# Casting weights inside their transfers: the last input-weight slice and all output weights go to fp16 on the way in, issued by GpSimd

## The chip, the cores and the metric

The kernel runs on one core of one Trainium2 chip. A core has a matrix engine (TensorE, PE in the profile), a vector engine (VectorE, DVE), an activation engine (ScalarE, ACT), a general engine (GpSimd, POOL) and a queue engine (SyncE, SP) that only issues transfers. ACT and POOL can issue transfers too, each on a queue of its own; all queues are worked off by the same 16 DMA engines. The metric is the device time of one execution in microseconds, taken as the median of several runs. A profile is one such execution, recorded.

## What is computed

A linear-attention recurrence (retention) over four batches of 768 tokens with 8 heads of 64, then one feed-forward block on all 3072 tokens. Cut to what matters:

```python
gamma = 1.0 - 2.0 ** (-5.0 - np.arange(H))          # H = 8, D = 64, S = 768, B = 4
for t in range(S):
    state = gamma * state + einsum('bhd,bhe->bhde', k[:, :, t], v[:, :, t])
    y[:, :, t] = einsum('bhd,bhde->bhe', q[:, :, t], state) / sqrt(D)
x = y.transpose(0, 2, 1, 3).reshape(B * S, H * D)    # 3072 x 512
h = x @ w_in                                         # w_in 512 x 2048
g = h * tanh(softplus(h))                            # mish
out = g @ w_out                                      # w_out 2048 x 512
```

All inputs and the output are fp32 in DRAM; the matrix products are done on fp16 operands.

## The kernel before

The tokens are cut into 24 chunks of 128 (a batch has six). A chunk's recurrence is done as matrices: scores k·q under a mask of decays (`scores`, `mask`), the outer product that updates the state (`outer`, `state`), and the output as a part from the present chunk and a part from the state (`present`, `past`, together `y_two`). For that q and k must lie transposed. Chunks 4 and 5 are turned by PE (`turn`), later ones by a transposing transfer (`turn_by_dma`). The casts of q and v to fp16, with the decay factors, are GpSimd's (`cast_q`, `cast_v`), that of k is ScalarE's (`cast_k`).

The feed-forward works in blocks. Block 0 has four chunks (512 tokens) and is done by plain products; the later ones have two chunks each. In block 0 the first product goes in 16 steps (`g1`, u = 0 to 15, four matmuls each, the two first in halves by `first_g1`), each followed by the mish activation on ScalarE; the second product has 16 steps more (`g2_mm`, w = u - 16, four matmuls each). From block 1 on (first product) and block 2 on (second product) a scheme with seven half-size products in place of eight is used, which needs sums and differences of weights, built once: `win_sums` from input-weight slices 0 and 2, `weight_sums` from output-weight slices 0 and 2 (half 0) and 1 and 3 (half 1). These are VectorE's, put in a list called `late` and taken from it at given places by `some_late`.

The weights come in slices. `w_in` has four slices of 512 columns (slice s serves steps u = 4s to 4s + 3, each of its two halves two steps). `w_out` has four slices of 512 rows (slice s serves w = 4s to 4s + 3). Before, each slice of 1 MiB is brought as fp32 into a staging buffer by SP's queue (`load_w`, L145 to L158; the last output slice in two halves by `load_last_wout`, L160 to L163) and cast to a resident fp16 tile: the first half slice by GpSimd, the other input slices and output slices 0 to 2 by VectorE (`cast_win`, L165; `cast_wout`, L171), output slice 3 by ScalarE. The staging pool has four buffers, also used by the first q and later by the sums, so a transfer may wait until a buffer's last reader is done. Output slices 2 and 3 are staged in another pool.

The order of all work is written by hand: each engine executes its instructions in the order in which the program names them, and waits by semaphores for what they read. What sets the order around the change:

- SP's queue at the start (`first_block`, L804): first q, the k and v of chunks 0 to 3, then `load_weights` (L777): the input slices, output slices 0 to 2, then q and v of chunk 4.
- The dictionary `plan` (L885): work to be named after step u of block 0. `load_more` (L787, after u = 15) issues k of chunk 4 and q and v of chunk 5 on ScalarE's queue, where they stand behind the activation of step 15, and on SP's queue k of chunk 5, the last output slice and the loads of chunks 6 and 7.
- The last lines of the loop over u (L914 to L918): the buffers of the weight sums and the sums themselves.

`gate` (L346) is a one-column copy by GpSimd into a scratch tile; it makes what follows on that queue wait for the tile that it reads.

```python
16: [(cast_wout, 2), (load_more,), (casts, CPB)],
23: [(casts, CPB + 1), (cast_wout, 3, True)],
24: [(turn, CPB)],
25: [(scores_one, CPB)],
27: [(turn, CPB + 1)],
```

Here CPB is 4: chunk 4 is turned after step u = 23, chunk 5 after u = 26.

Of the kernel before, what the change touches and what calls it, by code (L numbers as in the profile page):

```python
# [9 lines left out]
FP16 = mybir.dt.float16  # L10
FP32 = mybir.dt.float32
# [5 lines left out]
def kernel(  # L17
# [9 lines left out]
    nc = tc.nc  # L27
    B, H, S, D = q.shape
    d_model, d_ff = moe_w_in.shape
    P = 128  # L30
# [4 lines left out]
    TB = 512  # L35
    CPB = TB // C
# [4 lines left out]
    NFB = d_ff // P  # L41
# [41 lines left out]
    gcm = cpool.tile([P, HP, P], FP32, name="gcm")  # L83
    warm = cpool.tile([P, 1], FP32, name="warm")
    gate_t = cpool.tile([P, 1], FP16, name="gate")
    nc.gpsimd.memset(ident, 0.0)
    nc.gpsimd.affine_select(
        out=ident, in_=ident, compare_op=ALU.not_equal, fill=1.0, base=0,
# [53 lines left out]
            load(nload[0])  # L142
            nload[0] += 1

    def load_w(which, s):  # L145
        if which == "in":
            t = wstage.tile([P, NBP, TB], FP32, name="wi", tag="wt", bufs=4)
            n = TB // 2 if s < 2 else TB
            for o in range(0, TB, n):
                nc.sync.dma_start(t[:, :, o:o + n], win_ap[:, :, s * TB + o:s * TB + o + n])  # L150
        else:
            if s < NSL // 2:
                t = wstage.tile([P, FPS, d_model], FP32, name="wt", tag="wt", bufs=4)
            else:
                t = gp.tile([P, FPS, d_model], FP32, name="wt", tag="g")
            if s < NSL - 1:
                nc.sync.dma_start(t, wout_ap[:, s * FPS:(s + 1) * FPS])
        wtmps[which, s] = t  # L158

    def load_last_wout(half):  # L160
        f = slice(half * (FPS // 2), (half + 1) * (FPS // 2))
        nc.sync.dma_start(
            wtmps["out", NSL - 1][:, f], wout_ap[:, NFB - FPS + f.start:NFB - FPS + f.stop])  # L163

    def cast_win(s, half, eng):  # L165
        src = wtmps["in", s]
        t = cpool.tile([P, NBP, TB // 2], FP16, name=f"win{s}_{half}")
        eng.tensor_copy(t, src[:, :, half * (TB // 2):(half + 1) * (TB // 2)])
        wins[s, half] = t

    def cast_wout(s, on_act=False):  # L171
        src = wtmps.pop(("out", s))
        t = cpool.tile([P, FPS, d_model], FP16, name=f"wout{s}")
        if on_act:
            for f in range(0, FPS, 2):
                nc.scalar.copy(t[:, f:f + 2], src[:, f:f + 2])
        else:
            nc.vector.tensor_copy(t, src)
        wouts[s] = t

    def store(n):
        for _ in range(n):
# [163 lines left out]
    def gate(x):  # L346
        nc.gpsimd.tensor_copy(gate_t, x)  # L347
# [6 lines left out]
    def at_tile():  # L354
        return atps.tile([P, 2, HP // 2, R, C], FP32, name="at", tag="at")
# [180 lines left out]
    def some_late(n):  # L536
        for _ in range(min(n, len(late))):
            late.pop(0)()
# [236 lines left out]


    def load_weights():  # L777
        for s in range(NSL):
            load_w("in", s)
        for s in range(NSL):  # L780
            load_w("out", s)
        room(CPB)
        room(CPB + 1)
        load_one(CPB, 0, nc.sync)
        load_one(CPB, 2, nc.sync)

    def load_more():  # L787
        load_one(CPB, 1, nc.scalar)
        load_one(CPB + 1, 0, nc.scalar)
        load_one(CPB + 1, 2, nc.scalar)  # L790
        load_one(CPB + 1, 1, nc.sync)
        load_last_wout(0)
        load_last_wout(1)
        nload[0] += 2
        load_to(CPB + 4)

# [7 lines left out]
    def first_block():  # L804
# [49 lines left out]
        for half in range(2):  # L854
            cast_two("v", 1, half)
        cast_win(0, 0, nc.gpsimd)
        at = at_tile()
        scores_half(1, 1, at)
        mask_half(1, 1, at)
# [16 lines left out]
        state_first(3)  # L876
        for s in range(1, NSL):
            for half in range(2):
                cast_win(s, half, nc.vector)
            if s == 2:  # L880
                late.extend(win_sums())
            if s >= 2:
                some_late(4)
        room_for_sums()
        plan = {  # L885
            9: [(cast_wout, 0)],
            12: [(cast_wout, 1)],
            16: [(cast_wout, 2), (load_more,), (casts, CPB)],
            23: [(casts, CPB + 1), (cast_wout, 3, True)],
            24: [(turn, CPB)],  # L890
            25: [(scores_one, CPB)],
            27: [(turn, CPB + 1)],
# [5 lines left out]
        for u in range(2, 2 * NFB):  # L898
            if u < NFB:
                g1(0, u)  # L900
            elif u < 2 * NFB - 2:
                w = u - NFB
                for t in range(CPB):
                    if w == 0:
                        o_tiles[t] = mmps.tile([P, d_model], FP32, name="o_ps", tag="mm")
                    g2_mm(o_tiles[t], 0, t, w)
            else:
                for t in range(CPB // 2) if u % 2 == 0 else range(CPB // 2, CPB):
                    for w in range(NFB - 2, NFB):
                        g2_mm(o_tiles[t], 0, t, w)  # L910
                    g2_out(o_tiles[t], 0, t, 1, on_act=t == CPB - 1)
            for fn, *args in plan.get(u + 1, ()):
                fn(*args)
            if u == NFB - 1:  # L914
                room_for_more()
                late.extend(weight_sums(0) + weight_sums(1))
            if NFB <= u < NFB + 5:
                some_late(1)  # L918
        hsnaps.append(gp.tile([P, 4, TB], FP32, name="hsnap", tag="g0"))

# [122 lines left out]
```

## Time and profile before

| what | value |
|---|---|
| median of three runs | 204.29 us (203.35 to 204.36) |
| the profiled execution | 203.41 us |
| its span, first to last instruction | 201.2 us |
| PE busy | 193.6 us, 96% |
| VectorE, ScalarE, GpSimd busy | 142.3, 111.2, 68.1 us |
| transfers | 38.65 MB, mean 192 GB/s |
| granted PE clock | 1.000 |

In the profile's lines a group reads: line, engine, operation, output <- inputs, shapes and count. In a timeline each line starts with the start and the duration in microseconds, and ends, in brackets, with the idle time of the engine just before and with what ended it. SPq and ACTq are issues of transfers; the transfer itself lands later. In the table by stretches a row has the stretch, then PE's busy time, its count of matmuls, the granted clock, the DMA engines' share and GB/s. In the chart of 40 slices a digit is the busy share of a slice of 5 us in tenths.

### The profile page before, as it was taken

What the parts mean: (1) busy time and instruction counts of PE and PEld (TensorE: products, weight loads), DVE (VectorE), ACT (ScalarE), POOL (GpSimd) and SP (SyncE); (2) the same over time, 40 slices, a digit from 0 to 9 for tenths busy, and PEclk for the clock granted to TensorE, in tenths of its full rate; (3) what the DMA queues carried; (4) which work ended last, traced back from release to release, by engine and by line L of the source; (5) the groups of instructions that cost most, each with busy time, mean ns of one, the idle gap of its engine ahead of it and who ended that gap; (6) DMA issues with size and microseconds to landing.
All of it is one profiled execution on the core that took longest, in us unless ns stands there. A gap on an engine that the chain in (4) does not pass through costs nothing.

```text
span 201.2 us, 5425 instructions
## 1 busy us (share of the span) xinstructions
PE 193.6 (96%) x2239; PEld 152.5 (76%) x2239; DVE 142.3 (71%) x271; ACT 111.2 (55%) x199; POOL 68.1 (34%) x83
## 2 busy tenths in 40 slices
PE   6897999999999999999999999999999999999993
PEld 2355544455965888988988988988988988988982
DVE  2787793958839696787696695787696695595552
ACT  2363665243970874674674674674664763753840
POOL 4072000529324417514407607603406616200000
PEclk9999999999999999999999999999999999999999
DMA  5999999999999999997992993999993923200202
GB/s 169 302 312 359 385 387 302 271 263 205 210 180 269 279 221 195 199 227 166 215 194 72 232 230 73 232 190 153 241 200 57 235 81 55 104 3 30 79 26 78
DMA packets 95896, 38.65 MB, mean 192 GB/s; under 512 B 82304, under 2 KB 89984, under 8 KB 95872
## 3 DMA queue, kind: packets, MB, share of 16 engines
q1 hardware_dynamic: 92608, 37.50, 84.3%
q10 hardware_dynamic: 3264, 0.82, 2.3%
q8 instruction: 17, 0.28, 0.6%
q14 instruction: 7, 0.06, 0.1%
HBM read 27.30 MB, written 6.29 MB: 167 GB/s over the span
## 4 chain that ended last, share of the span: by engine, by line
PE 91%; ACT 2%; DMA 2%; DVE 2%; issue 1%; DVEq 0%
PE o_ps L727 28%; PE h_ps L656 18%; PE h_ps L632 16%; PE o_ps L519 10%; PE h_ps L497 6%; PE y_ps L436 3%; PE at L386 3%; DMA qfirst<-in_q_dram 2%; PE y_ps L426 2%; PE u_ps L400 2%; ACT xt L482 1%; PE h_ps L800 1%; DVE qfirst L204 1%; DVE am L274 1%; ACT qk L235 1%
## 5 line engine op out<-in xcount | busy, mean ns | idle before, releaser
L656 PE MATMUL h_ps<-xt,win 128*128 128x256 f16 x320 | 41.2, 273 | 0.0
L329 POOL TENSOR_TENSOR qk<-qf,qvs 128x512 f16<-128x512 f32 x20 | 24.1, 1207 | 25.3 <-DMA qf<-in_q_dram 23.4
L656 PEld LDWEIGHTS <-win 128*128 128x128 f16 x320 | 29.3, 98 | 3.7
L727 PEld LDWEIGHTS <-gsum 128*128 128x128 f16 x288 | 27.5, 98 | 4.0
L649 DVE TENSOR_TENSOR hsum<-h_ps,hsnap 128x512 f32<-128x512 f32 x30 | 19.8, 688 | 13.7 <-PE h_ps L632 11.5
L392 DVE TENSOR_TENSOR am<-at,tri 128x1024 f16<-128x1024 f32 x20 | 24.2, 1217 | 3.9 <-PE at L386 3.9
L660 ACT ACTIVATE g<-h_ps 128x512 f16<-128x512 f32 x40 | 23.7, 593 | 5.6 <-PE h_ps L656 5.5
L727 PE MATMUL o_ps<-tmat,gsum 128*128 128x256 f16 x216 | 25.1, 273 | 0.0
L639 ACT COPY hsnap<-h_ps 128x512 f32<-128x512 f32 x30 | 16.6, 588 | 13.9 <-PE h_ps L632 13.9
L338 POOL TENSOR_TENSOR v<-vf,qvs 128x512 f16<-128x512 f32 x20 | 21.3, 1064 | 5.3 <-PE u_ps L400 3.9
L727 PEld LDWEIGHTS <-g 128*128 128x128 f16 x216 | 21.1, 98 | 2.5
L741 DVE TENSOR_TENSOR osb<-o_ps,snap 128x256 f32<-128x256 f32 x27 | 11.4, 424 | 16.1 <-PE o_ps L727 11.3
L519 PE MATMUL o_ps<-wout,g 128*128 128x512 f16 x96 | 22.7, 380 | 0.0
L643 ACT ACTIVATE g<-hsum 128x512 f16<-128x512 f32 x30 | 18.7, 634 | 4.0 <-DVE hsum L649 4.0
L482 ACT CAST xt<-y_ps 128x1024 f16<-128x1024 f32 x10 | 10.1, 1012 | 19.1 <-PE y_ps L436 19.1
L632 PEld LDWEIGHTS <-wsum 128*128 128x128 f16 x320 | 19.1, 98 | 0.5
L733 ACT COPY snap<-o_ps 128x256 f32<-128x256 f32 x27 | 10.0, 372 | 15.7 <-PE o_ps L727 15.7
L334 ACT ACTIVATE qk<-kf 128x512 f16<-128x512 f32 x20 | 12.7, 633 | 8.4 <-DMA kf<-in_k_dram 8.4
L727 PE MATMUL o_ps<-wout,g 128*128 128x256 f16 x144 | 17.2, 273 | 0.0
L632 PE MATMUL h_ps<-xsum,wsum 128*128 128x128 f16 x240 | 16.7, 219 | 0.0
L347 POOL COPY gate<-gsum 128x1 f16<-128x1 f16 x8 | 1.5, 186 | 44.2 <-DVE gsum L701 44.2
L632 PEld LDWEIGHTS <-win 128*128 128x128 f16 x240 | 15.1, 98 | 1.5 <-issue 0.8
(96 smaller groups left out, 288.3 us busy)
## 6 DMA issues: line engine op xcount, KB each, us to landing
kf<-in_k_dram SPq DMA_DIRECT2D x23, 256.0 KB, 4.4
vf<-in_v_dram SPq DMA_DIRECT2D x23, 256.0 KB, 5.5
out_dram<-osb SPq DMA_DIRECT2D x22, 256.0 KB, 4.3
qf<-in_q_dram SPq DMA_DIRECT2D x19, 256.0 KB, 4.5
wt<-in_moe_w_out_dram SPq DMA_DIRECT2D x3, 1024.0 KB, 8.7
wi<-in_moe_w_in_dram SPq DMA_DIRECT2D x4, 512.0 KB, 7.2
wi<-in_moe_w_in_dram SPq DMA_DIRECT2D x2, 1024.0 KB, 11.1
qfirst<-in_q_dram SPq DMA_DIRECT2D x2, 512.0 KB, 5.2
```

The source lines that it names most:

```text
L329: nc.gpsimd.tensor_tensor(room16(g)[0], loaded[g][0], qs.unsqueeze(2).broadcast_to((P, H, D)), op=ALU.mult)
L334: nc.scalar.mul(room16(g)[1], loaded[g][1], BOOST)
L338: nc.gpsimd.tensor_tensor(room16(g)[2], loaded[g][2], vs.unsqueeze(2).broadcast_to((P, H, D)), op=ALU.mult)
L392: nc.vector.tensor_tensor(am, ats.pop(g), tri.unsqueeze(1).unsqueeze(1).broadcast_to((P, 2, HP, C)), op=ALU.mult)
L519: nc.tensor.matmul(o_ps, gts[blk, fb][:, t * P:(t + 1) * P], wouts[s][:, f, cols], start=(fb == 0), stop=(fb == NFB - 1))
L632: nc.tensor.matmul(h_ps[:, f], w(f, d), x(d), start=first and f == 0 and d == 0, stop=d == n - 1, skip_group_check=True)
L639: nc.scalar.copy(x, h_ps)
L643: nc.scalar.activation(gt[:, 2 * i * FPS:(2 * i + 1) * FPS, j * P:(j + 1) * P], h, AF.Mish, scale=inv_boost3)
L649: nc.vector.tensor_tensor(h, h_ps, x, op=ALU.add)
L656: nc.tensor.matmul(h_ps[:, j], win(s, 2 * half + j, bp), xt(blk, bp), start=bp == 0, stop=bp == NBP - 1)
L660: nc.scalar.activation(gt[:, fb:fb + 2], h_ps, AF.Mish, scale=inv_boost3)
L727: nc.tensor.matmul(o_ps, x(f), w(f), start=first and f == 0, stop=f == n - 1, skip_group_check=True)
```

## The change

A transfer that GpSimd issues may change the type of what it moves. The change uses this for the last input slice (two transfers, one per half) and for all four output slices: the fp16 tiles are written by the transfers directly, with no staging buffer and no cast by an engine.

On GpSimd's queue, behind the cast of the first half slice, stands a gate on the second half of input slice 1; then the two halves of input slice 3 and output slices 0, 2 and 1, in this order. Output slice 3 is issued after step u = 15, between the cast of q and that of v of chunk 4. On SP's queue, behind input slice 2, stands a transfer of one element out of output slice 2's tile (`gate_d`), so that the loads of q and v of chunk 4, now named in `load_more`, and all behind them wait for that slice. The sums of output slices 0 and 2 are named after step u = 11 (four at once), those of slices 1 and 3 from step u = 24 on.

```diff
+    gate_d = cpool.tile([1, 1], FP16, name="gate_d")
...
-    def load_w(which, s):
...
-    def load_last_wout(half):
...
+    def load_win(s):
+        t = wstage.tile([P, NBP, TB], FP32, name="wi", tag="wt", bufs=4)
+        n = TB // 2 if s < 2 else TB
+        for o in range(0, TB, n):
+            nc.sync.dma_start(t[:, :, o:o + n], win_ap[:, :, s * TB + o:s * TB + o + n])
+        wtmps[s] = t
+
+    def bring_win(s, half):
+        t = wins[s, half] = cpool.tile([P, NBP, TB // 2], FP16, name=f"win{s}_{half}")
+        o = s * TB + half * (TB // 2)
+        nc.gpsimd.dma_start(t, win_ap[:, :, o:o + TB // 2])
+
+    def bring_wout(s):
+        t = wouts[s] = cpool.tile([P, FPS, d_model], FP16, name=f"wout{s}")
+        nc.gpsimd.dma_start(t, wout_ap[:, s * FPS:(s + 1) * FPS])
...
-    def cast_wout(s, on_act=False):
...
     def load_weights():
-        for s in range(NSL):
-            load_w("in", s)
-        for s in range(NSL):
-            load_w("out", s)
+        for s in range(NSL - 1):
+            load_win(s)
+
+    def bring_weights():
+        gate(wtmps[1][:, 0, TB // 2:TB // 2 + 1])
+        for half in range(2):
+            bring_win(NSL - 1, half)
+        for s in (0, 2, 1):
+            bring_wout(s)
+
+    def load_more():
+        nc.sync.dma_start(gate_d, wouts[2][:1, 0, :1])
         room(CPB)
         room(CPB + 1)
         load_one(CPB, 0, nc.sync)
         load_one(CPB, 2, nc.sync)
-
-    def load_more():
         load_one(CPB, 1, nc.scalar)
         load_one(CPB + 1, 0, nc.scalar)
         load_one(CPB + 1, 2, nc.scalar)
         load_one(CPB + 1, 1, nc.sync)
-        load_last_wout(0)
-        load_last_wout(1)
         nload[0] += 2
         load_to(CPB + 4)
...
         cast_win(0, 0, nc.gpsimd)
+        bring_weights()
...
         for s in range(1, NSL):
             for half in range(2):
-                cast_win(s, half, nc.vector)
+                if s < NSL - 1:
+                    cast_win(s, half, nc.vector)
...
         plan = {
-            9: [(cast_wout, 0)],
-            12: [(cast_wout, 1)],
-            16: [(cast_wout, 2), (load_more,), (casts, CPB)],
-            23: [(casts, CPB + 1), (cast_wout, 3, True)],
+            16: [(load_more,), (cast_q, CPB), (bring_wout, NSL - 1), (cast_k, CPB), (cast_v, CPB)],
+            23: [(casts, CPB + 1)],
...
-            if u == NFB - 1:
+            if u == NFB - 5:
                 room_for_more()
-                late.extend(weight_sums(0) + weight_sums(1))
-            if NFB <= u < NFB + 5:
+                late.extend(weight_sums(0))
+                some_late(4)
+            if u == NFB + 8:
+                late.extend(weight_sums(1))
                 some_late(1)
```

More of the change, by code (lines that the diff above doesn't have):

```diff
@@ L143, in load_to @@
             nload[0] += 1
-    def load_w(which, s):
[L146 to L158, printed above, removed]
-    def load_last_wout(half):
-        f = slice(half * (FPS // 2), (half + 1) * (FPS // 2))
-        nc.sync.dma_start(
-            wtmps["out", NSL - 1][:, f], wout_ap[:, NFB - FPS + f.start:NFB - FPS + f.stop])
+    def load_win(s):
[11 more added lines that the diff above has]
+        nc.gpsimd.dma_start(t, wout_ap[:, s * FPS:(s + 1) * FPS])
     def cast_win(s, half, eng):
-        src = wtmps["in", s]
+        src = wtmps[s]
         t = cpool.tile([P, NBP, TB // 2], FP16, name=f"win{s}_{half}")
@@ L169, in cast_win @@
         wins[s, half] = t
-    def cast_wout(s, on_act=False):
[L172 to L179, printed above, removed]
     def store(n):
```

## The prediction, made before the result was known

> **What bounds the kernel now.** I read the page first: the share of each engine and the 40 slices. Then TensorE's (PE's) busy time by stretches, PE's timeline from 20 to 50 us, and last the queues and casts that feed it. From the page:
>
> ```profile
> span 201.2 us, 5425 instructions
> PE 193.6 (96%) x2239; PEld 152.5 (76%) x2239; DVE 142.3 (71%) x271; ACT 111.2 (55%) x199; POOL 68.1 (34%) x83
> DMA  5999999999999999997992993999993923200202
> ```
>
> PE is busy 96% of the span, and the DMA engines are full from 5 to about 90 us. By stretches (us, PE busy and matmuls, granted clock, DMA share, GB/s):
>
> ```profile
> 20.00:50.00 30.00, 29.96 (x190) 1.00 1.12 304
> 50.00:100.00 50.00, 49.73 (x609) 1.00 1.13 219
> 100.00:150.00 50.00, 50.00 (x637) 1.00 0.99 181
> ```
>
> From 20 to 150 us PE idles 0.04 + 0.27 + 0 = 0.31 us. The rest of its idle time lies before 20 us, ahead of the first new instruction (it waits for a transfer that lands at 20.8), or behind the last matmul. So the change can win 0.3 us at most, and can lose whatever it makes PE wait. The question is when each operand comes. PE's timeline (start, duration, us) says when it is wanted:
>
> ```profile
> 20.98 12.25 PE L497 MATMUL h_ps<-xt,win 128*128 128x512 f16 x56
> 33.07 7.27 PE L519 MATMUL o_ps<-wout,g 128*128 128x512 f16 x32
> 40.17 0.39 PE L373 MATMUL t_ps<-ident,qk 128*128 128x128 f16 x4
> 43.65 0.39 PE L373 MATMUL t_ps<-ident,qk 128*128 128x128 f16 x4
> 45.18 1.03 PE L519 MATMUL o_ps<-wout,g 128*128 128x512 f16 x4
> ```
>
> A step u of four matmuls takes 12.1/14 = 0.86 us, so win3 is wanted at 20.98 + 10 x 0.86 = 29.6 (u = 12), its second half at 31.4; wout0 at 33.07, wout1 (w = 4) at 33.07 + 4 x 0.89 = 36.6, wout2 (w = 8) at 40.6, wout3 at 45.18. The turns at 40.17 and 43.65 want q and k of chunks 4 and 5, cast. The supply of today, from the timelines of VectorE (DVE), GpSimd (POOL) and ScalarE (ACT):
>
> ```profile
> 21.79 1.28 DVE L168 CAST win<-wi 128x1024 f16<-128x1024 f32 x2
> 23.47 1.29 DVE L168 CAST win<-wi 128x1024 f16<-128x1024 f32 x2 [0.40 <-DMA wi<-in_moe_w_in_dram]
> 29.08 1.23 DVE L178 CAST wout<-wt 128x2048 f16<-128x2048 f32 x1
> 31.78 1.23 DVE L178 CAST wout<-wt 128x2048 f16<-128x2048 f32 x1 [1.47 <-DMA wt<-in_moe_w_out_dram]
> 34.60 1.23 DVE L178 CAST wout<-wt 128x2048 f16<-128x2048 f32 x1 [1.59 <-DMA wt<-in_moe_w_out_dram]
> 35.80 1.53 POOL L329 TENSOR_TENSOR qk<-qf,qvs 128x512 f16<-128x512 f32 x1 [19.01 <-DMA qf<-in_q_dram]
> 39.76 0.63 ACT L334 ACTIVATE qk<-kf 128x512 f16<-128x512 f32 x1 [1.01 <-DMA kf<-in_k_dram]
> 43.53 1.04 ACT L176 CAST wout<-wt 128x1024 f16<-128x1024 f32 x1 [0.66 <-DMA wt<-in_moe_w_out_dram]
> ```
>
> Each cast starts as its transfer lands. The margins are small: wout0 is done at 30.3 (2.8 us early), wout1 at 33.0 (3.6), wout2 at 35.8 (4.8), k5 at 40.4 (3.3), wout3 at 44.6 (0.6). The stage is paid for in DMA time, and has about 1 us to spare.
>
> **The change, part by part.** *Removed:* five DVE casts (3 x 1.23 + 2 x 0.69 = 5.1 us) and two ACT casts (2 x 1.04 = 2.1 us). Neither engine bounds PE after 20 us, so I count 0 for them and keep the 0.3 us as the other end; the cover, PE's own matmuls, stays. Each of these weights comes a cast earlier for the same landing.
>
> *SP's queue:* six weight transfers leave it (win3, wout0 to wout2, two halves of wout3). A one-element transfer (gate_d) enters that waits for wout2. Behind it stand q4, v4, k5, and all of chunks 6 and 7: today q4 and v4 are issued at 24.9 and 25.6, ahead of any wait for wout2. gate_d's own bytes are nothing; its wait is counted below. ACT's loads (k4, q5, v5) still go out at 33.3 with the last activation of the first matrix product.
>
> *GpSimd's queue:* a gate of one column (0.19 us, by the gates of the page's lines at L347) waits for the second half of the second slice, issued at 12.37 and landed 8.4 us later, 20.8. Then come five transfers, cast_q of chunk 4, wout3's transfer, and the other casts. Today POOL idles from 16.8 to 35.8, so the gate delays nothing by itself. But wout3 now stands behind cast_q, which waits for q4, which waits for wout2.
>
> No row shows the writing of a transfer by GpSimd. Nearest below: 0.4 us, an issue by ACT (kf, 33.27). Nearest above: 1.36 us, a part of the three L157 issues on SP that took 4.45 with their waits. I take 1.0, the time of POOL's own pass over such a tile (1.04). Its start beside the DVE casts at 21.79 and 23.47 may cost more: POOL's cast_q took 1.53 beside two-input DVE work and 1.04 alone.
>
> *Bytes:* the third slice's transfer (issued 13.25, landed 10.2 later, 23.45) keeps the DMA engines fed until about 22.9; with 21.0 for the gate and 1.0 to 3 for the first transfer I take a hole of 1.2 us (ends: 0 and 4). No row shows a transfer that casts. Plain ones of this shape run at 388 GB/s (25 to 30 us), 2.7 us a MiB; a cast reads the same bytes and writes half. Ends: 2.0 us (three quarters of the bytes) and 5.4 us (half the rate). I take 2.7, the row of the same read.
>
> Then, last bytes plus 0.6 us to landing: win3 at 24.1 + 2.7 = 26.8 + 0.6 = 27.4, wout0 30.1, wout2 32.8, wout1 35.5. All are before their time (29.6, 33.07, 40.6, 36.6): no stall yet, with 1.1 us left at wout1.
>
> *The loads behind:* at 33.4 q4 starts, instead of standing queued. From there until all is in: the rest of wout1 (1.5 us), six loads of chunks 4 and 5 at 256 KB / 220 GB/s = 1.19 each (7.1), wout3 (2.7), 0.6 to landing: 33.4 + 11.9 = 45.3. Which comes last is set by turns between queues. Today v5 on ACT's queue, beside wout3's rows on SP's, landed 4.9 us after q5 (33.72 + 6.7 = 40.4; 34.36 + 11.0 = 45.4), four times its 1.19: one 256-byte row gets its turn per 2 KB row. After the change wout3 has a queue of its own and starts about 40 (q4 landed 37.5, cast_q 1.53, writing 1.0), just when k5, third on SP's queue, comes up. So k5 pays what v5 pays today. It lands between 42.6 (wout3 after it) and 46; I take 45.5, nearest to the v5 row, since only q6 can share the rest. With 0.75 us for ACT's cast and the signal it is ready at 46.3; the turn wanted it at 43.65: PE waits about 2.7 us. wout3 (about 4 us for 1 MiB in turns, 44.6) then costs nothing more.
>
> *Sum:* the profiled execution, 203.41 (span 201.2, 2.2 around it), - 0 + 2.7 = 206.1 us. The runs' median of 204.29 lies 0.9 above this execution; the range covers it. A measurement of this kernel tells 0.5% (1.0 us) from no change.
>
> *A rule of the notes against the row.* The row: a MiB of weights lands 2.7 us after the one before (29.08 to 31.78). The Trainium skill, DMA: Bandwidth & Descriptors, section Measured (HBM→SBUF, 128 partitions, SWDGE, issued from GpSimd), gives 79 us for 16 MB from this queue, so by estimate 4.9 us a MB. By that the sum would be near 215; it speaks for the second rival, and no run here shows it yet.
>
> **The rivals.**
> (1) *Hidden, no change:* if the hole is 0 and the turns favour k5, k5 lands at 42.6 and PE waits for nothing: 203.1 to 204.4. For it: wout3 gains 1.04 us by losing its last cast, and 3 to 5 us of margin stand in every other weight. Against: the DMA engines are full on both sides, and SP's loads start later. It decides from k5 landing before 42.9.
> (2) *Casting transfers are slower.* At 4 us a MiB, four MiB lie from win3's start (24.1) to wout1, which lands at 24.1 + 16 + 0.6 = 40.7, 4.1 late, and what stands behind it (k5, wout3 with its own 1.3) pushes the turn to about 7 us late: 210. At 5.4 us, wout1 is 9.7 late, and the loads another 3 to 5: 216 to 218. For it: a different descriptor writer and a conversion, which no row shows. Against: the read side is the same.
> (3) *DVE holds up the transfers' writing.* DVE casts run from 21.79 to 23.07 and from 23.47 to 24.76, just when GpSimd writes. If it stands still for both, the hole is 1.2 + 2.6 = 3.8 us; wout1 comes 1.5 late and k5 about 5: 208.5. For it: POOL's 1.53 for 1.04. Against: those were two-input reads on DVE, not casts. The Trainium skill, SBUF — State Buffer, box The "DVE blocks DMA" trap (SWDGE), says just this of fp32 copies by VectorE. The reverse also: win1's cast has only 0.2 us to spare (PE waited that long for it), and each 1 us of a held port there costs PE about 0.8.
> (4) *Faster:* only if casting transfers cost by what they write; then everything is early, and PE's last 0.3 us go: 203.1, under what can be told.
>
> **How the numbers follow.** My forecast (k5 late, 1 to 4 us; own range 204.5 to 207.5) 45%; hidden 23%; slow casting 17%; DVE hold 11%; faster 4%. The predicted time is the first, 206.1. The range runs from 203.2 (the lower part of hidden, and faster, left out: about 8%) to 213 (slow casting beyond 4.6 us a MiB left out: about 10%). Slower by over 0.5%: 45 + 17 + 11 = 73, less 2 for a k5 that is late by under 1 us, 71%. Same: 23 + 2 less 1 = 24%. Faster: 4 + 1 for a run that falls low, 5%.
>
> **What would show it.** Right: PE idle in 20 to 50 us grows from 0.04 to about 2.7, in front of the second turn (its line among the waits, released by ACT's cast of k5, itself by its DMA); wout0 to wout2 land in steps of 2.7 us from about 30; DVE idles where the L178 casts stood. wout1 as the releaser of an o_ps matmul at w = 4 with steps over 4 us says rival 2; a hole in the DMA row between 22 and 25 us with such steps of 2.7 says rival 3; PE idle under 0.5 us says rival 1. A PE clock under 1.00 after a stall would add to any of them, and nothing here prices that. The prediction is wrong if the wait falls before 33 us, or past 50, where chunks 6 and 7 (landed at 49 to 51 today, read by SP's transposes from 48.0) come later still.

## The result, and the profile after

The changed kernel takes 207.31 us (median of four runs, 205.57 to 208.44), the kernel before 204.12 in the same session: a ratio of 1.0156, with an interval of 1.0122 to 1.0190. It is slower by about 3 us. Where single executions of a version ran over 1.5% longer than its fastest, its median and ratio here are taken without them. The profiled execution took 206.96 us, its span 205.2. In two of the four runs the mean granted clock of TensorE was 1.00 (206.96 and 205.57 us), in the other two 0.992 (208.44 and 207.67).

From the page of the changed kernel: the span, the busy times and the DMA row of the 40 slices.

```profile
span 205.2 us, 5424 instructions
PE 194.1 (95%) x2239; PEld 153.2 (75%) x2239; DVE 138.6 (68%) x266; ACT 109.2 (53%) x197; POOL 72.3 (35%) x90
...
DMA  5999899999999999999997894999991972200102
```

DVE fell from 142.3 to 138.6 us and ACT from 111.2 to 109.2. PE has the same 2239 matmuls and half a microsecond more of busy time. The saved casts bought nothing, since neither engine set PE's pace (PE had idled 0.04 us from 20 to 50 us). In the DMA row the fifth slice (20.5 to 25.6 us), a 9 before, is now an 8.

PE's busy time by stretches of the changed kernel (us, busy and matmuls, granted clock, DMA share, GB/s):

```profile
20.00:50.00 30.00, 27.10 (x156) 1.00 1.10 192
50.00:100.00 50.00, 49.73 (x592) 1.00 1.27 212
100.00:150.00 50.00, 50.00 (x651) 1.00 1.03 187
```

The loss inside the kernel's body lies in 20 to 50 us: PE idles 2.90 us there, where it idled 0.04. Of the 4.0 us by which the span grew, 0.50 is a later start (the first long run of matmuls begins at 21.48 instead of 20.98; in the executions recorded below it begins between 20.20 and 20.98 too, so this differs from one to the next), and 0.45 lies behind the last matmul. The time outside the span shrank, from 2.2 to 1.8 us. PE begins the next block at 54.12 instead of 50.49. PE's timeline of the changed kernel shows where it stands still (start, duration, then in brackets the idle time before and what ended it):

```profile
33.56 7.27 PE L506 MATMUL o_ps<-wout,g 128*128 128x512 f16 x32
...
42.36 0.40 PE L360 MATMUL t_ps<-ident,qk 128*128 128x128 f16 x4 [1.53 <-POOL qk L316]
...
45.85 0.39 PE L360 MATMUL t_ps<-ident,qk 128*128 128x128 f16 x4
...
48.81 1.02 PE L506 MATMUL o_ps<-wout,g 128*128 128x512 f16 x4 [1.27 <-DMA wout<-in_moe_w_out_dram]
```

Output slices 0, 2 and 1 come in time: 32 matmuls, those of slices 0 and 1, run on without a wait at 33.56. Slice 1 has 0.1 us to spare (landed at 37.00, wanted at 37.1); slice 2, landed at 34.04, is first read at 42.82. There are two waits, and both stand on GpSimd's queue. At the first turn PE waits 1.53 us for GpSimd's cast of q of chunk 4 (q4). At the last four slice steps it waits 1.27 us for output slice 3, whose transfer GpSimd writes behind that cast. The second turn, at 45.85, waits for nothing. GpSimd's timeline of the changed kernel:

```profile
21.02 0.19 POOL L334 CAST gate<-wi 128x1 f16<-128x1 f32 x1 [3.99 <-DMA wi<-in_moe_w_in_dram]
21.14 2.13 POOL L156 DMA_DIRECT2D win<-in_moe_w_in_dram  x2
23.26 2.39 POOL L160 DMA_DIRECT2D wout<-in_moe_w_out_dram  x3
41.27 1.04 POOL L316 TENSOR_TENSOR qk<-qf,qvs 128x512 f16<-128x512 f32 x1 [15.62 <-DMA qf<-in_q_dram]
42.26 0.81 POOL L160 DMA_DIRECT2D wout<-in_moe_w_out_dram  x1
```

The cast waits 15.62 us for q4 and starts when it lands. Slice 3's transfer, written at 42.26, lands at 48.77. SP's queue (SPq) says why q4 is late:

```profile
34.06 0.73 SPq L776 DMA_DIRECT2D gate_d<-wout  x1
34.84 0.38 SPq L133 DMA_DIRECT2D qf<-in_q_dram  x1
```

The one-element transfer is issued when output slice 2 has landed (34.04). q4 follows at 34.84, was at 24.92 before, and lands at 41.19, before at 35.73. One stage earlier stands the reason why slice 2 is late. DMA share and GB/s per microsecond (the last two columns), first of the kernel before, then of the changed one:

```profile
22.00:23.00 1.00, 1.00 (x7) 1.00 1.05 385
23.00:24.00 1.00, 1.00 (x6) 1.00 1.07 389
```

```profile
21.00:22.00 1.00, 1.00 (x8) 1.00 0.65 229
22.00:23.00 1.00, 1.00 (x7) 1.00 0.23 54
23.00:24.00 1.00, 1.00 (x6) 1.00 1.26 162
24.00:25.00 1.00, 1.00 (x7) 1.00 0.90 117
```

From 21 to 23 us the DMA engines lie idle for 0.35 + 0.77 = 1.1 us. The gate opens at 21.02 and the first packet of a casting transfer starts at 22.79, while what SP had queued ran dry. (From 23 us on the GB/s count the fp16 bytes that are written, half of what is read.)

### The profile page after: what moved, and what is told of

It is laid out like the page before. It is cut to its first block, busy times and chain, and to the rows that moved or that the text cites. A ratio compares the mean times of both kernels' runs of the same rounds, so it can differ in the third digit from the quotient of the medians.

```text
span 205.2 us, 5424 instructions
## 1 busy us (share of the span) xinstructions
PE 194.1 (95%) x2239; PEld 153.2 (75%) x2239; DVE 138.6 (68%) x266; ACT 109.2 (53%) x197; POOL 72.3 (35%) x90
## 4 chain that ended last, share of the span: by engine, by line
PE 73%; DMA 15%; SPq 6%; POOL 2%; ACT 1%; issue 1%; DVE 0%
PE o_ps L714 27%; PE h_ps L643 17%; PE h_ps L619 16%; DMA wout<-in_moe_w_out_dram 8%; PE o_ps L506 4%; DMA wi<-in_moe_w_in_dram 4%; SPq L211 4%; DMA qf<-in_q_dram 3%; PE y_ps L423 3%; PE at L373 3%; PE y_ps L413 2%; PE u_ps L387 2%; SPq L150 1%; POOL win L156 1%; ACT xt L469 1%
## 5 line engine op out<-in xcount | busy, mean ns | idle before, releaser
L643 PEld LDWEIGHTS <-win 128*128 128x128 f16 x320 | 29.4, 98 | 3.6
L316 POOL TENSOR_TENSOR qk<-qf,qvs 128x512 f16<-128x512 f32 x20 | 23.4, 1169 | 20.4 <-DMA qf<-in_q_dram 20.4
L714 PEld LDWEIGHTS <-g 128*128 128x128 f16 x216 | 21.2, 98 | 2.4
L506 PEld LDWEIGHTS <-g 128*128 128x128 f16 x96 | 8.8, 98 | 11.1 <-issue 1.7
```

What stands on the lines that cost most here:

```text
L316: nc.gpsimd.tensor_tensor(room16(g)[0], loaded[g][0], qs.unsqueeze(2).broadcast_to((P, H, D)), op=ALU.mult)
L506: nc.tensor.matmul(o_ps, gts[blk, fb][:, t * P:(t + 1) * P], wouts[s][:, f, cols], start=(fb == 0), stop=(fb == NFB - 1))
L643: nc.tensor.matmul(h_ps[:, j], win(s, 2 * half + j, bp), xt(blk, bp), start=bp == 0, stop=bp == NBP - 1)
L714: nc.tensor.matmul(o_ps, x(f), w(f), start=first and f == 0, stop=f == n - 1, skip_group_check=True)
```

## The experiments

The theory from these readings: a casting transfer costs what a plain one costs, and the loss is place in a stretch in which the DMA engines have no time to give: the hole behind the gate, which moves everything after it, and the order of the loads behind output slice 2. The rivals: conversion within a transfer is slow; VectorE's casts hold up GpSimd's writing; the one-element gate or slice 3's place alone is to blame. The kernel before took 203.75 to 203.85 us (medians) in all the sessions below.

**The hole, smaller and larger.** The gate on GpSimd was moved to an earlier and to a later landing. Earlier, on the first half of input slice 1:

```diff
-        gate(wtmps[1][:, 0, TB // 2:TB // 2 + 1])
+        gate(wtmps[1][:, 0, :1])
```

> GpSimd's gate is on the first half of input slice 1 (landed 19.6) in place of the second (landed 21.0). Theory (order): the hole of about 1.3 us in the DMA engines between 21.8 and 23.0 closes, the cast transfers start about 1.3 us earlier and everything behind them, q4 and output slice 3 too, comes 1 to 1.3 us earlier; the two waits shrink from 2.8 to 0.5 to 1: 205.0. Input slice 2 shares and lands up to 0.5 us later, which nobody waits for. Rival (port: VectorE's casts hold up GpSimd's writing of the transfers): the writing now falls beside other VectorE casts and the hole stays or grows, 206.5 to 207.5.

It took 205.05 us, ratio 1.0078 [1.0047, 1.0109], as the theory had it (205.0). GpSimd writes from 20.16, the DMA share in 21 to 22 us is 0.87 instead of 0.65 and in 22 to 23 it is 1.10 instead of 0.23, output slice 2 lands at 32.73 instead of 34.04, and PE idles 1.86 us in 20 to 50: 1.3 for output slice 3 and 0.5 for ScalarE's cast of k5 at the second turn. The wait for q4 is gone.

Later, on input slice 2:

```diff
-        gate(wtmps[1][:, 0, TB // 2:TB // 2 + 1])
+        gate(wtmps[2][:, 0, :1])
```

> The changed kernel with GpSimd's gate on input slice 2 (landed 23.6) in place of the second half of slice 1 (21.0): the hole in the DMA engines is made longer by 2.65 us. Theory (order): every microsecond of hole is a microsecond for PE, since the stage has nothing left to spare: 207.3 + 2.65 = about 210. Rival (port: VectorE's casts hold up GpSimd's writing): the casts of slices 1 and 2 are over by 24.8, so the transfers are written faster, and the loss against the changed kernel stays under 1 us, under 208.3.

It took 209.62 us, ratio 1.0326 [1.0263, 1.0389]. From 24 to 25 us not one byte moves; from 21 to 26 us the engines lie idle for 4.2 us, where it was 1.1. PE's waits in this kernel:

```profile
31.87 1.90 PE L484 MATMUL h_ps<-xt,win 128*128 128x512 f16 x8 [0.89 <-DMA win<-in_moe_w_in_dram]
34.69 3.63 PE L506 MATMUL o_ps<-wout,g 128*128 128x512 f16 x16 [0.91 <-DMA wout<-in_moe_w_out_dram]
40.42 5.30 PE L506 MATMUL o_ps<-wout,g 128*128 128x512 f16 x16 [2.11 <-DMA wout<-in_moe_w_out_dram]
```

Now the weights themselves are late, input slice 3 first. GpSimd wrote these two halves in 1.68 us (24.22 to 25.90), and VectorE's last fp32 cast ended at 24.84, so hardly any writing was left for VectorE to hold up; by that rival this kernel would have been no slower than 208.3. Earlier gate, the change, later gate: 205.05, 207.31, 209.62. Against the kernel before in the session of each, that is 1.3, 3.2 and 5.8 us more.

**One part of the change alone.** The output slices only: input slice 3 is staged on SP and cast by VectorE, as before.

```diff
-        for s in range(NSL - 1):
+        for s in range(NSL):
             load_win(s)
...
-        for half in range(2):
-            bring_win(NSL - 1, half)
         for s in (0, 2, 1):
...
-                if s < NSL - 1:
-                    cast_win(s, half, nc.vector)
+                cast_win(s, half, nc.vector)
```

> The output slices' half of the change alone: all four input slices are staged on SP's queue and cast by VectorE as before; GpSimd still writes the casting transfers of output slices 0, 2, 1 behind the same gate, and slice 3 behind cast_q of chunk 4. Theory (the loss is a place in full DMA time: a hole behind the gate, and loads held behind output slice 2): SP's queue now holds 1 MiB more when the gate opens, so there is no hole; all transfers behind it come about 1.3 us sooner than in the changed kernel, q4 is issued near 32.5 to 33.5 instead of 34.84, and what is left is a wait of up to 1.3 us for output slice 3. Expected 204.3 to 205.3 us. Rival (two queues sharing the DMA engines delay whichever the kernel wants first): input slice 3 shares with output slice 0, lands up to 2.7 us later than before and stops PE between 29 and 32 us: 206 to 207.5 us.

It took 203.79 us (ten runs), ratio 1.0008 [0.9992, 1.0024]: level with the kernel before. DMA share and GB/s per microsecond, and PE's timeline, of this kernel:

```profile
22.00:23.00 1.00, 1.00 (x6) 1.00 1.12 406
23.00:24.00 1.00, 1.00 (x7) 1.00 1.00 371
```

```profile
39.72 0.39 PE L360 MATMUL t_ps<-ident,qk 128*128 128x128 f16 x4
...
46.19 1.02 PE L506 MATMUL o_ps<-wout,g 128*128 128x512 f16 x4 [1.30 <-DMA wout<-in_moe_w_out_dram]
```

There is no hole: input slice 3's MiB on SP's queue covers the gate and the writing of the first transfer. Output slices 0, 2 and 1 land at 28.58, 31.20 and 34.03, q4 is issued at 32.01, and only the wait for output slice 3 is left. The rival is refuted: input slice 3 lands at 26.21, at 26.34 in the kernel before. That execution took 204.27 us, 0.48 above the median of its kernel, which lies under the expected 204.3 to 205.3; what its other executions waited for is not recorded. So the larger part of the loss comes in with input slice 3. This run changes two things there at once, the hole and slice 3's short rows, which take longer (see the last section); the two moved gates change the hole and leave the rows as they are.

Input slice 3 only, in the kernel before; the output slices are staged and cast as before:

```diff
     def load_weights():
-        for s in range(NSL):
+        for s in range(NSL - 1):
             load_w("in", s)
...
+    def bring_win3():
+        gate(wtmps["in", 1][:, 0, TB // 2:TB // 2 + 1])
+        for half in range(2):
+            t = wins[NSL - 1, half] = cpool.tile([P, NBP, TB // 2], FP16, name=f"win3_{half}")
+            o = (NSL - 1) * TB + half * (TB // 2)
+            nc.gpsimd.dma_start(t, win_ap[:, :, o:o + TB // 2])
...
-                cast_win(s, half, nc.vector)
+                if s < NSL - 1:
+                    cast_win(s, half, nc.vector)
```

> The kernel before with one part of the change: input slice 3 alone is cast in its transfers, behind the same gate; the output slices stay on SP's queue with VectorE's and ScalarE's casts. Theory (order, by turns): output slice 0's 2 KB rows on SP's queue now run beside input slice 3's 1 KB ones, 64 pairs of 64 + 88 ns = 9.7 us from 22.8, so the second half lands at about 33 in place of 27.2, wanted at 31.4: PE waits about 1.6 us at u = 14 and the rest follows: 205.3. Rival (turns do not matter, the engines share by bytes): no wait, 203.6 to 203.9.

It took 209.03 us, ratio 1.0259 [1.0244, 1.0274], 3.7 more than expected. PE's waits in this kernel:

```profile
30.94 1.90 PE L497 MATMUL h_ps<-xt,win 128*128 128x512 f16 x8 [1.94 <-DMA win<-in_moe_w_in_dram]
34.81 3.04 PE L497 MATMUL h_ps<-xt,win 128*128 128x512 f16 x8 [1.97 <-DMA win<-in_moe_w_in_dram]
46.28 0.40 PE L375 MATMUL t_ps<-ident,qk 128*128 128x128 f16 x4 [0.76 <-ACT qk L334]
```

The output slices stand on SP's queue right behind input slice 2 and keep the engines fed, but they take turns with input slice 3, which PE wants first: its halves land at 30.89 and 34.77, in the changed kernel at 25.42 and 27.18. My expectation had these turns, with the second half at about 33 and one wait of 1.6 us; it had left out that the first half comes late too. After the second wait eight matmuls took 3.04 us, and eight take 1.90 at the full clock: the granted clock over 20 to 50 us is 0.94. The two parts of the change do not add up: alone one costs nothing and the other 5.3 us, together they cost 3.2.

**Conversion or queue.** The same transfers on the same GpSimd queue behind the same gates, but in fp32 into staging, with the casts back on VectorE and ScalarE. The edit is shown against the kernel before; the sums of weights stay where that kernel has them:

```diff
+            if s == NSL - 1:
+                n = TB // 2
+            queue = nc.gpsimd if s == NSL - 1 else nc.sync
             for o in range(0, TB, n):
-                nc.sync.dma_start(t[:, :, o:o + n], win_ap[:, :, s * TB + o:s * TB + o + n])
+                queue.dma_start(t[:, :, o:o + n], win_ap[:, :, s * TB + o:s * TB + o + n])
...
-            if s < NSL - 1:
-                nc.sync.dma_start(t, wout_ap[:, s * FPS:(s + 1) * FPS])
+            nc.gpsimd.dma_start(t, wout_ap[:, s * FPS:(s + 1) * FPS])
...
-            16: [(cast_wout, 2), (load_more,), (casts, CPB)],
+            16: [(load_more,), (cast_wout, 2), (cast_q, CPB), (load_w, "out", NSL - 1), (cast_k, CPB), (cast_v, CPB)],
```

> The transfers stay on GpSimd's queue, in the same order, with the same gate and the same one-element transfer, but move fp32 into staging buffers, and VectorE and ScalarE cast as before the change. Theory (order): the loads of chunk 4 and output slice 3 are as late as in the changed kernel, and each slice pays its cast on top (1.23 for slice 1, wanted at 37.1 and landed at 37.0; 1.04 for the end of slice 3): 206.96 + 1 to 2 = 208 to 209. Rival (conversion): without conversion the packets are as fast as on SP's queue (88 in place of 107 ns, 52 in place of 64 ns for input slice 3: 96 x 19 + 64 x 12 = 2.6 us), the waits go and the time comes back to 204 to 205.

It took 212.48 us, ratio 1.0432 [1.0405, 1.0459]. Its output slices land at 31.83, 34.54 and 37.34, in steps of 2.71 and 2.80; those of the changed kernel at 31.53, 34.04 and 37.00, in steps of 2.51 and 2.96. Taking the conversion away wins no time for the output slices. (The profile shows the plain transfers on this queue in packets of 4 KB, so this compares landings, not rows.) What makes this kernel 5 us slower than the changed one is on PE's timeline and on VectorE's:

```profile
33.13 3.63 PE L518 MATMUL o_ps<-wout,g 128*128 128x512 f16 x16 [0.39 <-DVE wout L177]
38.65 3.61 PE L518 MATMUL o_ps<-wout,g 128*128 128x512 f16 x16 [1.89 <-DVE wout L177]
...
48.57 0.61 PE L385 MATMUL at<-qkt 64*128 64x128 f16 x8 [4.47 <-DVE qkt L376]
```

```profile
39.65 0.69 DVE L550 TENSOR_TENSOR tmat<-wout 128x1024 f16<-128x1024 f16 x1
...
43.03 4.88 DVE L550 TENSOR_TENSOR tmat<-wout 128x1024 f16<-128x1024 f16 x1
47.83 0.68 DVE L376 COPY qkt<-t_ps 128x1024 f16<-128x1024 f16 x1
```

Two of the waits, 0.39 and 1.89 us, are for casts of slices that come late. So much is the cast within the transfer worth once the slices are late; it was worth nothing while they came early. The longest wait, 4.47 us, is not for a cast. The copy that PE needs (qkt) stands on VectorE behind a sum of weights that took 4.88 us, where one of the same line and shape took 0.69. Beside it GpSimd's casts of q and v run without a gap, from 43.32 to 47.35. So the 5 us are not the price of the casts, and of the conversion the run shows only that the slices land no sooner without it.

**The loads behind output slice 2.** Without the one-element transfer SP's loads go out behind the input slices at once:

```diff
     def load_more():
-        nc.sync.dma_start(gate_d, wouts[2][:1, 0, :1])
         room(CPB)
```

> The one-element transfer that makes SP's loads wait for output slice 2 is taken out; all else as in the changed kernel (profiled execution 206.96 us; PE waits 1.5 us for cast_q of chunk 4 and 1.3 us for output slice 3). Theory (order: the loss comes from where transfers stand, q4 behind output slice 2 and output slice 3 behind cast_q): q4, v4, k5 and chunks 6 and 7 now flow from about 23 us in turns with the weights, one 256-byte row of some 22 ns per weight packet, 160 packets up to output slice 1, so that slice lands 3.5 us later (37.0 to 40.5, wanted at 37.1). Both old waits vanish and one of about 3.4 us appears at w = 4: 206.96 - 2.8 + 3.4 = 207.5. Rival (conversion: casting transfers themselves are dear, the order does not matter): the wait in front of the turn of chunk 4 stays or moves by under 0.5 us, time within 0.5 us of 206.96. Either way it should not come back to 204.

It took 207.57 us (median of three runs), ratio 1.0193 [1.0145, 1.0242]: as slow as the change, and as the theory had it. So the one-element gate is not what makes the change slow. That the wait moved to w = 4 is not shown: the recorded execution took 397.35 us, with PE's matmuls about twice as long as elsewhere, and no wait is read from it.

Output slice 3 ahead of the cast of q4 on GpSimd:

```diff
-            16: [(load_more,), (cast_q, CPB), (bring_wout, NSL - 1), (cast_k, CPB), (cast_v, CPB)],
+            16: [(load_more,), (bring_wout, NSL - 1), (cast_q, CPB), (cast_k, CPB), (cast_v, CPB)],
```

> Output slice 3's transfer is issued before cast_q of chunk 4 on GpSimd's queue, not behind it. Theory (order): it then follows output slice 1 directly, from 37 us, lands by 41 and PE's wait of 1.3 us for it at 48.8 vanishes; but q4's rows take turns with it, 32 packets of 98 ns more, so the wait in front of the turn of chunk 4 grows from 1.5 to about 4 us: 206.96 - 1.4 + 2.5 = 208. Rival (the two waits are independent, so that early issue is free): 206.96 - 1.4 = 205.6.

It took 208.56 us, ratio 1.0255 [1.0217, 1.0292]. PE's wait in this kernel:

```profile
43.67 0.40 PE L360 MATMUL t_ps<-ident,qk 128*128 128x128 f16 x4 [3.42 <-POOL qk L316]
```

Slice 3 lands at 39.87, 9 us earlier, and its wait is gone, but its MiB now stands ahead of q4, which lands at 42.50. Two waits of 1.5 and 1.3 became one of 3.4. The two are not independent costs; they share one supply.

q4 ahead of the gates, as it was before the change:

```diff
             load_win(s)
+        room(CPB)
+        room(CPB + 1)
+        load_one(CPB, 0, nc.sync)
...
         nc.sync.dma_start(gate_d, wouts[2][:1, 0, :1])
-        room(CPB)
-        room(CPB + 1)
-        load_one(CPB, 0, nc.sync)
```

> The changed kernel with one load moved: q of chunk 4 is issued on SP right behind input slice 2, ahead of gate_d, so its 256 KB stand queued when the gate opens. Theory (place in DMA time): the 256 KB fill most of the hole of 1.3 us and cost the weights at most 0.6 us; cast_q of chunk 4 is done before 30 us and output slice 3's transfer is written by 28 us, directly behind slice 1, landing near 40. Both of the changed kernel's waits (1.5 us for cast_q at the first turn, 1.3 us for slice 3) go; what comes last is now k of chunk 4 or 5 on the queues behind slice 3, with 0.5 to 1.5 us of wait at a turn. Expected 204.6 to 205.8 us. Rival (it is the bytes of slice 3 ahead of the turns that cost, as where slice 3 was written ahead of cast_q): k of chunk 4 comes as late as q did there, PE waits over 3 us: 207 to 208.5 us.

It took 205.45 us, ratio 1.0097 [1.0066, 1.0129], within the expected range. Its recorded execution is a longer one (206.77), with a wait of 2.23 us where 0.5 to 1.5 was expected; the waits of the shorter ones are not recorded. PE's timeline:

```profile
42.25 0.40 PE L362 MATMUL t_ps<-ident,qk 128*128 128x128 f16 x4 [2.23 <-ACT qk L321]
...
44.12 3.13 PE L506 MATMUL o_ps<-wout,g 128*128 128x512 f16 x8
```

Both old waits are gone (the cast of q4 starts at 25.73, slice 3 lands at 40.03), and k4 is late in their place: it landed at 38.09 in the changed kernel and lands at 41.54 here, behind slice 3. Again the clock falls behind the wait (eight matmuls in 3.13 us).

**The way back.** The earlier gate, and the one-element gate on output slice 0 instead of 2, so that the loads start sooner:

```diff
-        gate(wtmps[1][:, 0, TB // 2:TB // 2 + 1])
+        gate(wtmps[1][:, 0, :1])
...
-        nc.sync.dma_start(gate_d, wouts[2][:1, 0, :1])
+        nc.sync.dma_start(gate_d, wouts[0][:1, 0, :1])
```

> As gate_early (median 205.05), and the one-element transfer on SP's queue waits for output slice 0 in place of slice 2. Theory (order): the loads of chunk 4 are issued at about 31 in place of 33.5; taking turns with the weights' 1 KB packets they gain about half of it, q4 lands 1.3 us earlier, GpSimd issues output slice 3 at 38.5 in place of 39.8, and PE's last wait (1.3 us for slice 3) shrinks to 0 to 0.3; output slice 1 lands 1 us later, at 36.3, just in time. 203.9 to 204.3, level with the kernel before. Rival (the first part of the loss, the late q4, was all that mattered, slice 3 waits for something else): 204.8 to 205.3.

Its median is 204.28 us (seven runs, 203.89 to 204.79; two more took 207.30 and 208.27), its ratio 1.0027 [1.0016, 1.0039]: within the expected range, and most of the loss is back. The same with the output slices in the order 0, 1, 2:

```diff
-        for s in (0, 2, 1):
+        for s in (0, 1, 2):
```

> As early_d0, with output slices brought in the order 0, 1, 2. Theory (order): slice 1 lands at about 33 and slice 2 at 36.5, both well ahead of PE (36.6 and 40.6); q4 and slice 3 as in early_d0. So the same as early_d0 within 0.3 us if slice 1 was in time there, and up to 0.5 us faster if it was not: 203.8 to 204.2. No theory expects it under 203.4.

204.00 us (ten runs, 203.57 to 206.60), ratio 1.0027 [1.0000, 1.0054]. The recorded executions of both are among their longest (207.30 and 206.60 us), and both show the same wait, which therefore is not that of the median. PE in the first of them:

```profile
47.60 1.02 PE L506 MATMUL o_ps<-wout,g 128*128 128x512 f16 x4 [2.53 <-DMA wout<-in_moe_w_out_dram]
48.56 0.61 PE L373 MATMUL at<-qkt 64*128 64x128 f16 x8
49.10 3.27 PE L506 MATMUL o_ps<-wout,g 128*128 128x512 f16 x8
```

Slice 3's transfer is written at 37.35 and lands at 47.56. Its first packet moves at 41.4 us. No version beats the kernel before; three (these two and the output slices alone) come within 0.3% of it.

## Why the prediction came out as it did

The prediction said 206.1 us, and slower with a chance of 0.71. Measured: 207.31.

*Cast removal counted as 0.* Right. DVE and ACT are 3.7 and 2.0 us less busy (5.1 and 2.1 were counted) and PE gains nothing from it.

*The hole of 1.2 us.* Right in size, 1.1 us, and 1.3 us earlier than I had put it: I had SP's queue feeding the engines until 22.9, and they run dry between 21 and 22. It is what the loss hangs on: against the kernel before of the same session, a smaller hole costs 1.9 us less than the change, one longer by 3.1 us costs 2.6 more, and the variant without one is level with before.

*Writing a transfer, 1.0 us each.* Measured 0.94, 1.20, 0.80, 0.81, 0.80 and, at 42.26, 0.81. Right enough.

*Casting transfers, 2.7 us a MiB.* Right for the output slices (2.51 and 2.96 from one landing to the next). Mis-sized for input slice 3: it comes in halves, and a half's row is 1 KB where the whole slice's was 2 KB. Such a packet took 64 ns on the mean, a 2 KB one 88.6 in the kernel before (20 to 30 us), so a KB costs 64 instead of 44, and the packets of this MiB run for 4.1 us (from 22.79 to 26.88), where 2.7 was counted. The second half landed at 27.18, as forecast (27.4), only because the first packet came at 22.79 instead of 24.1. The output slices then landed at 31.53, 34.04 and 37.00 against 30.1, 32.8 and 35.5, some 1.2 to 1.5 us late. The 16 engines finish one of these transfers 1.8 to 2.4 us apart, and a landing is the last one's; I had added 0.6 to the last bytes.

*Loads start at 33.4; "gate_d's own bytes are nothing".* Half right. SP could go on at 34.06, and 0.73 us went on issuing that element, so q4 went out at 34.84. I had also q4 landed at 37.5; it landed at 41.19.

*The second turn waits 2.7 us for k5.* Here the prediction failed in place. k5 landed at 44.61, not 45.5, and was cast at 45.27. The second turn stood at 45.85, 2.2 us later than before, and found it ready: the lateness of k5 lay hidden behind that of q4. ScalarE's timeline of the changed kernel has k4 and k5 at

```profile
38.11 0.63 ACT L321 ACTIVATE qk<-kf 128x512 f16<-128x512 f32 x1 [3.75 <-DMA kf<-in_k_dram]
...
44.64 0.63 ACT L321 ACTIVATE qk<-kf 128x512 f16<-128x512 f32 x1 [5.89 <-DMA kf<-in_k_dram]
```

The wait came one turn earlier, for q4, which I had passed as in time; its margin is not even among those that I listed (its cast was done at 37.33, wanted at 40.17). The step that failed is the sharing of the engines: "one 256-byte row gets its turn per 2 KB row". I reckoned with sharing for k5, and let q4 land 4.1 us after its start. It took 6.35 us (34.84 to 41.19), beside the end of output slice 1 and ACT's loads of k4 and q5: half of the 16 engines had finished it at 39.23, the last one at 41.19. Nor are the turns single rows; the last section has their length in another kernel.

*wout3 "costs nothing more".* Wrong. I had it start at 40 and land at 44.6. q4's lateness moved the start to 42.26, and it landed at 48.77, 1.27 us too late for its four matmuls.

*The sum.* I forecast 2.7 us of PE waits and there were 1.53 + 1.27 = 2.80, at other places. That the size agrees is luck for the most part: the place was wrong, and the sum lacked three smaller terms: 0.50 of later start, 0.45 behind the last matmul, and 1.8 us around the span where I had kept 2.2. It is not luck that the change loses: in four kernels with the same gate (the change, slice 3 first, q4 first, no one-element gate) the waits that were recorded move between q4, k4 and slice 3, and each of the four is slower than the kernel before, by 1.6 to 4.8 us.

*A clock under 1.00 after a stall,* which I had named and not priced: it is there. In two of the change's four runs the mean clock was 0.992. These two average 208.1 us, the two without it 206.3. A stretch of 3.41 us at half the clock could make up to 1.7 us of that, so it may be why the median lies 1.2 above the forecast. Two runs against two that differ by 0.8 and 1.4 us among themselves do not show it, and the fall need not add to the time: with input slice 3 alone the execution with one took 209.07 us, the three without 208.75 to 209.13.

*Rival (1), hidden:* refuted for the whole change, and true for its half: the output slices alone are hidden (203.79). *Rival (2), slow casting:* refuted by steps that equal those of plain transfers on the same queue, and of those on SP's queue in the kernel before (2.70 and 2.82 us). The rule weighed against the row in the prediction, 79 us for 16 MB (the Trainium skill, DMA: Bandwidth & Descriptors, section Measured), does not hold for this kernel: two output slices land 2.5 and 3.0 us behind the one before, where its time makes 4.9. The same row's rate, 425 GB/s, makes 2.5 by estimate, and with that the trace agrees. *Rival (3), VectorE holds up the writing:* refuted as a price of 2.6 us. The sign that I had named for it, a hole in the DMA row with steps of 2.7 us behind it, did come, and does not tell it from my own forecast. Here is VectorE in the changed kernel:

```profile
22.29 3.06 DVE L165 CAST win<-wi 128x1024 f16<-128x1024 f32 x4
```

The transfers that GpSimd writes during these casts took 1.20 us (it overlaps the first), 0.80 and 0.81, and with VectorE idle 0.81. At most 0.4 us can be put down to it, once. The Trainium skill's box The "DVE blocks DMA" trap (SWDGE) (SBUF — State Buffer) describes a full stop of this writing beside VectorE's fp32 copies; these rows show none beside fp32 to fp16 casts.

*What stays open:* why the variant with the output slices alone is level in its median although its one recorded execution has 1.30 us of PE wait. Part of it lies outside the span: time less span is 2.15 us in the kernel before and 1.8 in this one, so its median span is longer, 202.0 us against 201.7. What was saved there is not recorded.

## What to carry to other kernels

Before a transfer is moved to another queue behind a gate, ask what the DMA engines still hold when the gate opens: gate plus first packet cost 1.8 us here, and one MiB left on the old queue covered all of it. In a stretch where the engines are full, what one operand gains another loses, so sum up the bytes that must be in by each use, and look at the first use, not at the operand that was last before. Casting in the transfer cost no transfer time for rows of 2 KB, but it is worth only what the engines that it relieves kept waiting, which was nothing here.

## What the runs showed of the hardware

- **Queues take long turns.** In the kernel with the one-element gate on slice 0, packets by queue (q1 is SP's, q10 ACT's) in 37 to 38, then in 39 to 40 us:

```profile
q10 hardware_dynamic: 840, 0.21, 131.5%
q1 hardware_dynamic: 26, 0.01, 3.9%
```

```profile
q1 hardware_dynamic: 858, 0.22, 134.2%
q10 hardware_dynamic: 2, 0.00, 0.3%
```

  Both queues had issued loads not yet landed all the while, and one of them got a whole microsecond. The turns are longer than that window: ACT's queue moves 2080 packets between 35.4 and 39.1 us and SP's 2080 between 37.8 and 41.5, which is 130 on each of the 16 engines, or two whole loads of 256 KB. (From 36.64 to 37.82 us SP's queue has not one packet; the engines change over at different times, so the two stretches overlap.) So a share by single rows, as I used, does not forecast a landing. The Trainium skill (DMA: Bandwidth & Descriptors, section Queues, rings and completion order) says that an engine drains a batch of about 9 to 17 descriptors, 64 at most, from one queue before it goes on to the next. If a packet of the profile is one descriptor, the turns here are twice that ceiling. In 41 to 43 us of the kernel before the two queues had 819 and 796 packets, and no such turns can be told apart.
- **A wait costs clock when enough of it falls into one stretch of 3.41 us.** PE's rows in the kernel with the one-element gate on slice 0, then in the one with slice 3 first:

```profile
45.10:48.51 3.41, 0.91 (x4) 1.00 0.96 193
48.51:51.92 3.41, 3.41 (x16) 0.50 1.05 194
```

```profile
38.53:41.95 3.42, 1.72 (x8) 1.00 1.32 240
41.95:45.36 3.41, 1.69 (x20) 1.00 1.34 216
```

  In all eleven recorded executions that have a record of the clock, it changes only at borders 3.41 us apart, or a multiple of it, and where they lie differs from one execution to the next. At full clock, a stretch between two borders in which PE idled 1.97 us or more (1.97, 2.11, 2.16, 2.23, 2.51 and 3.41 us in six executions) was followed by one at half the clock; none with 1.94 us or less was (idle time by PE's modelled ends). The wait of 3.42 us with slice 3 first was cut by a border into 1.70 and 1.72 us, and cost no clock. The Trainium skill (TensorE: Matmul & The Clock Gate, section Part 1: The HAM clock gate (the "warmup" mystery)) has a free-running window of 3.4 us and half the clock after an idle one. The borders agree with that; a window did not have to be wholly idle here, 58% of it (1.97 us) was enough.
- **A sum on VectorE can stand still beside GpSimd.** The sum of weights that takes 0.69 us took 4.88 beside four casts of GpSimd without a gap (plain transfers), and 2.32 in the changed kernel, from 45.36 to 47.68, where GpSimd's casts end at 47.12. Each sum reads two operands.
- **Casting by a transfer is free for long rows, and short rows are dear.** A packet that read 2 KB and wrote 1 KB took 98 ns (median) against 88 for a plain one of 2 KB; the landings came at the same pace. A packet that read 1 KB and wrote 512 bytes took 64 ns on the mean, a plain 1 KB one 52.
